# Filter weights queued ahead of two late tables, one activation table, and a first evacuation shared by two engines, in a spectral filter plus feed-forward kernel

## The chip, the cores and the metric

The kernel runs on one core of a Trainium2 chip. The metric is device microseconds for one execution, lower is better. The "span" of a profile is the part between the first and the last instruction of the core; the time of the same execution is 1.8 to 2.5 us longer in the executions quoted here. A run that is over 1.5% slower than the fastest of its kernel counts as slow: medians and ranges below include it, ratios leave it out, and no profile shown is of such a run. The engines are named as the profile names them: PE is the matrix engine (TensorE), DVE is VectorE, ACT is ScalarE, POOL is GpSimd, SP issues nearly all DMAs. A PSUM bank is one of the eight areas (0 to 7 in the zones of this kernel) that PE writes into and that ACT or DVE empties ("evacuates") before this kernel lets PE use it again.

## The reference, cut to what matters

```python
def reference(A_x, A_w_r, A_w_i, B_x, B_w1, B_b1, B_w2, B_b2):
    def _A_ref(x, w_r, w_i):                      # spectral filter
        X = jnp.fft.rfft2(x.astype(jnp.float32), axes=(-2, -1))
        X = X * (w_r + 1j * w_i)                  # filter weights: 2048 x 321, real and imaginary
        return jnp.fft.irfft2(X, s=(S, D), axes=(-2, -1)).astype(jnp.bfloat16)
    def _B_ref(x, w1, b1, w2, b2):                # feed-forward layer, 640 -> 1536 -> 640
        h = _gelu(jnp.einsum("bsd,df->bsf", x, w1) + b1)
        return jnp.einsum("bsf,fd->bsd", h, w2) + b2
    x = A_x                                       # 1 x 2048 x 640, bfloat16
    xn = _layernorm(x, axis=-1)
    return x + _A_ref(xn, A_w_r, A_w_i) + _B_ref(xn, B_w1, B_b1, B_w2, B_b2)
```

## The kernel before

The Fourier transforms are matrix products with constant tables (`gtab`, `etab`, `mtab` forward; `ntab`, `getab`, `htab` back). The sequence is cut into 16 chunks of 128 rows. A "ring" at the start normalises and transposes the chunks; blocks of chunks then go through the hidden layer (`ps<-xnT,W` in the profile, 128, 256 or 512 columns wide), and in between eight pairs go through forward transform, middle transform, multiplication with the filter weights and inverse transform. The names to know are `Xb` (a forward transform's result, evacuated), `Y` (a middle transform's result, evacuated), `T` (products of `Y` and the weights `Wf`), `Z` (their sums), and `Zs` (a rearranged part of `Z`, the "gather").

The program doesn't write the engines' orders by hand. Every operation gets a priority and a list of engines, a small model of the chip simulates the run, and the order that comes out of it is fixed for each engine. On the chip every engine goes through its own list in that order. No instruction passed a waiting one in front of it: in run 2 below, a copy on DVE that needs no weights starts at 59.23 us, behind products that waited 4.08 us for theirs.

```python
PRIO = {"hps": 10, "gelu": 50, "pb": 70, "pc": 80, "filt": 85, "ipc": 90, "xb": 20, "eps": 60, "fin": 40, "fst": 5}
WARM = 12          # matmuls that only bring PE's clock up
DEPTH = 4          # filter loads in flight at once
# ... cut ...
def schedule(self):
    # ... cut: the model; among the operations that could start now, the highest priority is taken
        t, o = min((c for c in cands if c[0] <= t0 + 0.03), key=lambda c: (-c[1].prio, c[1].seq))
# ... cut: the queue of loads, in program order: x chunks between three slabs of W1 (640 KB each) ...
load_x(0, 1)
load_x(1, 1)
load_w1(0)
load_w1(1)
load_x(2, 2)
load_w1(2)
# ... cut: the other x chunks, tables G, E, M, N, GE ...
load(b2bc[:], ...)                                   # bias broadcast, 160 KB
def load_w(dst, src, nbytes, rate):                  # one filter load waits for the one DEPTH before it,
    few.append(load(dst, src, B_w, nbytes, after=few[-DEPTH:][:1], rate=rate))   # or for the first one
# ... cut: 18 filter loads ...
load(htab[:]..., const["H"], B_h, 524288)            # table H, needed late
# ... cut ...
# the products wait for Y, for all filter loads, and for the end of the ring
t_ops[pair].append(K.op([("dve", ...)], pr, lambda e, _: e.tensor_tensor(out=T, in0=Y, in1=Wf, op=ALU.mult),
    reads=[Y, B_w, B_wpad], writes=[TB], after=ring_ops))
```

## Time and profile before

| what | before |
|---|---|
| time, first session | 164.24 us median of 4 runs |
| span of the profile that is read | 162.5 us |
| PE busy | 151.2 us, 93% |
| PE's largest waits after its first matmul | 2.70, 1.08, 0.81, 0.75, 0.55, 0.52, 0.42 us |

PE is the engine to shorten. Read its timeline as a list of waits: each has a length in brackets and the engine or transfer that ended it. The lines themselves stand in the prediction. One more fact matters for reading every comparison: the kernel before isn't steady. Its runs in four sessions range from 162.2 to 168.1 us with medians of 164.2, 166.2, 165.5 and 165.2. So a kernel is compared only with the runs of its own session.

### The profile page before, as it was taken

What the parts mean: (1) busy time and instruction counts of PE and PEld (TensorE: products, weight loads), DVE (VectorE), ACT (ScalarE), POOL (GpSimd) and SP (SyncE); (2) the same over time, 40 slices, a digit from 0 to 9 for tenths busy, and PEclk for the clock granted to TensorE, in tenths of its full rate; (3) what the DMA queues carried; (4) which work ended last, traced back from release to release, by engine and by line L of the source; (5) the groups of instructions that cost most, each with busy time, mean ns of one, the idle gap of its engine ahead of it and who ended that gap; (6) DMA issues with size and microseconds to landing.
All of it is one profiled execution on the core that took longest, in us unless ns stands there. A gap on an engine that the chain in (4) does not pass through costs nothing.

```text
span 162.5 us, 3629 instructions
## 1 busy us (share of the span) xinstructions
PE 151.2 (93%) x1485; PEld 96.7 (59%) x1485; DVE 122.4 (75%) x263; ACT 77.5 (48%) x156; POOL 30.7 (19%) x33
## 2 busy tenths in 40 slices
PE   6979899999999849889999989899999999999993
PEld 2469887455565333445454657567776667777771
DVE  3687999999964655969494999788999898932221
ACT  3098887786787365797769383333011103100000
POOL 1201211111000000000000000305965833333300
PEclk9999999999999978999999999999999999999999
DMA  4999949999999600005050400101344443111121
GB/s 122 355 380 397 300 127 159 169 70 141 127 103 144 146 4 0 0 4 161 4 161 8 160 0 0 38 6 42 108 138 119 131 155 120 45 40 40 42 74 47
DMA packets 18632, 17.84 MB, mean 110 GB/s; under 512 B 6713, under 2 KB 17337, under 8 KB 18489
## 3 DMA queue, kind: packets, MB, share of 16 engines
q1 hardware_dynamic: 18448, 17.59, 47.9%
q8 instruction: 11, 0.18, 0.5%
q10 hardware_dynamic: 168, 0.04, 0.1%
q14 instruction: 5, 0.03, 0.1%
HBM read 13.69 MB, written 2.62 MB: 100 GB/s over the span
## 4 chain that ended last, share of the span: by engine, by line
PE 60%; DVE 25%; ACT 7%; DMA 5%; issue 2%; SPq 0%; DVEq 0%
PE ps L478 59%; DMA Wf<-in_A_w_i_dram 5%; DVE T L627 4%; DVE stats L573 4%; DVE T L711 3%; DVE T L592 2%; DVE Z L716 2%; ACT Xb L485 2%; ACT Zs L485 2%; DVE Y L623 1%; DVE XW L488 1%; DVE Y L488 1%; PE ps L600 1%; ACT gT L655 1%; DVE T L623 1%
## 5 line engine op out<-in xcount | busy, mean ns | idle before, releaser
L478 PE MATMUL ps<-xnT,W 128*128 128x512 bf16 (+2 forms) x360 | 58.1, 311 | 2.1 <-ACT gT L655 2.0
L478 PE MATMUL ps<-W,gT 128*128 128x320 bf16 x384 | 56.3, 299 | 0.1
L478 PEld LDWEIGHTS ps<-W,gT 128*128 128x128 bf16 x384 | 36.7, 98 | 14.9 <-issue 0.5
L478 PEld LDWEIGHTS ps<-xnT,W 128*128 128x128 bf16 x360 | 29.0, 98 | 20.9 <-ACT gT L655 3.8
L655 ACT ACTIVATE gT<-ps,b1col 128x512 bf16<-128x512 f32 (+2 forms) x72 | 36.2, 549 | 8.4 <-PE ps L478 7.9
L821 POOL TENSOR_TENSOR xo<-xr,b2bc 128x640 f32<-128x640 bf16 x11 | 16.6, 1514 | 23.2 <-DVE ost L834 23.2
L485 ACT ACTIVATE Wf<-ps 128x640 bf16<-128x640 f32 x10 | 6.8, 702 | 27.1 <-PE ps L478 27.1
L821 POOL TENSOR_TENSOR xnT<-xr,xnT 128x640 f32<-128x640 bf16 x5 | 7.8, 1553 | 63.3 <-DVE Z L716 61.4
L834 DVE TENSOR_TENSOR ost<-ps,xo 128x640 bf16<-128x640 f32 (+1 forms) x12 | 9.2, 766 | 13.5 <-PE ps L478 13.4
L573 DVE BATCH_NORM_STATS2 stats<-XV 128x6 f32<-128x320 bf16 x32 | 14.1, 471 | 2.2 <-DMA XV<-in_A_x_dram 2.2
L711 DVE TENSOR_TENSOR T<-Y,Wf 128x1288 bf16<-128x1288 bf16 x16 | 12.7, 829 | 3.5 <-DMA Wf<-in_A_w_i_dram 3.0
L581 POOL TENSOR_TENSOR rstd<-ve,mhalf 128x2 f32<-128x2 f32 (+1 forms) x9 | 6.1, 681 | 33.8 <-DVE ve L580 33.8
L488 DVE CAST Y<-ps 128x644 bf16<-128x644 f32 x8 | 6.6, 827 | 6.4 <-PE ps L478 6.4
L804 DVE TENSOR_TENSOR Wf<-Wf 128x640 bf16<-128x640 bf16 x16 | 9.8, 642 | 1.4 <-ACT Wf L485 1.3
L809 DVE TENSOR_TENSOR Wf<-Wf 128x640 bf16<-128x640 bf16 x16 | 10.4, 676 | 0.1
L485 ACT ACTIVATE Zs<-Z 128x128 bf16<-128x128 bf16 (+1 forms) x32 | 6.0, 261 | 9.2 <-DVE Z L716 9.2
L488 DVE CAST XV<-ps 128x640 bf16<-128x640 f32 x8 | 6.6, 823 | 4.9 <-PE ps L478 4.9
L478 PE MATMUL ps<-ntab,Z 64*128 64x128 bf16 x128 | 5.4, 228 | 4.8 <-ACT Xb L485 4.0
L485 ACT ACTIVATE Xb<-ps 128x640 bf16<-128x640 f32 x10 | 8.5, 881 | 1.2 <-PE ps L478 1.2
L478 PEld LDWEIGHTS ps<-ntab,Z 64*128 64x128 bf16 x128 | 4.0, 100 | 8.1 <-ACT Xb L485 6.3
L478 PE MATMUL ps<-etab,XW 128*128 128x160 bf16 (+1 forms) x128 | 8.6, 234 | 0.0
L478 PE MATMUL ps<-getab,XV 128*128 128x160 bf16 (+1 forms) x128 | 8.6, 233 | 0.0
(48 smaller groups left out, 147.8 us busy)
## 6 DMA issues: line engine op xcount, KB each, us to landing
W<-in_B_w_dram SPq DMA_DIRECT2D x6, 640.0 KB, 5.1
xr<-in_A_x_dram SPq DMA_DIRECT2D x16, 160.0 KB, 2.3
out_dram<-ost SPq DMA_DIRECT2D x15, 160.0 KB, 1.8
XV<-in_A_x_dram SPq DMA_DIRECT2D x7, 320.0 KB, 9.1
Wf<-in_A_w_r_dram SPq DMA_DIRECT2D x7, 160.5 KB, 6.0
Wf<-in_A_w_i_dram SPq DMA_DIRECT2D x7, 160.5 KB, 5.4
gtab<-c_G SPq DMA_DIRECT2D x1, 512.0 KB, 8.4
htab<-c_H SPq DMA_DIRECT2D x1, 512.0 KB, 11.6
```

The costliest lines, as they stand in the source:

```text
L478: ins = e.matmul(o_, lhsT=lw, rhs=rh, start=st, stop=sp_)
L485: return e.activation(dst(), src(), ACT.Copy, scale=scale)
L488: return e.tensor_copy(dst(), src())
L573: K.op([("dve", 0.4)], 100 - c, lambda e, _, c=c, h=h: e.bn_stats(stats[:, c, 6 * h:6 * h + 6], view(XV, c * D + H2 * h, [[1, H2]])), read ...
L581: K.op([("pool", 0.75)], 100 - c, lambda e, _, a=a, b=b: e.tensor_tensor(out=rstd[:, a:b], in0=ve[:, a:b], in1=mhalf[:, a:b], op=ALU.pow), ...
L627: K.op([("dve", dve_us(4 * n, 2))], prf, lambda e, _, op=op, x1v=x1v, xfv=xfv, o_=o_, o0=o0, o1=o1, n=n: e.tensor_tensor(out=xfv(o_, [[D, ...
L655: K.op([("act", act_us(s1 - s0, 1))], pr + PRIO["gelu"], lambda e, _, s0=s0, s1=s1, fc=fc, hps=hps: e.activation(gT[:, fc, s0:s1], ps(hps. ...
L711: t_ops[pair].append(K.op([("dve", dve_us(4 * KP, 2))], pr, lambda e, _, k=k, Y=Y, TB=TB, pair=pair: e.tensor_tensor(out=view(TT, TB.slot ...
L804: K.op([("dve", dve_us(D, 2))], pr + 2, lambda e, _, k=k, op=op, yo=yo, y2=y2: e.tensor_tensor(out=view(Wf, Y2 + y2.slot * 2 * D + (H2 - 1 ...
L809: K.op([("dve", dve_us(D, 2))], pr + 3, lambda e, _, k=k, op=op, y2=y2, yf=yf: e.tensor_tensor(out=view(Wf, YF + yf.slot * 2 * D + (D - 1) ...
L821: K.op([("pool", pool_us(640))], 50, lambda e, _, c=c, xr=xr, xov=xov: e.tensor_tensor(out=xov(0, D), in0=halves(xrt[:, xr.slot, :]), in1= ...
L834: os_ops.append(K.op([("dve", dve_us(H2 * len(hs)))], 95, lambda e, _, a=a, b=b, hs=hs, xov=xov, fps=fps, os_=os_: e.tensor_tensor(out=hal ...
```

## The change

The intent: take the waits out of PE's row. The 18 filter loads go ahead of table H and the bias, and the first four of them go without waiting. A GELU on one column of a constant (128x1), as ACT's first instruction, loads the one table that both GELU and copy use. The first two chunks are transposed in two parts (three and two column blocks), one emptied by DVE and one by ACT. Two warm-up matmuls go, the second chunk's statistics wait for the first chunk's variance, and all priorities and bank zones get new values, which rearranges every engine's order. The core of the diff:

```diff
-PRIO = {"hps": 10, "gelu": 50, "pb": 70, "pc": 80, "filt": 85, "ipc": 90, "xb": 20, "eps": 60, "fin": 40, "fst": 5}
+PRIO = {'hps': 37.4, 'gelu': 82.7, 'pb': 120.8, 'pc': 154.1, 'filt': 90.5, 'ipc': 148.4, 'xb': 65.5, 'eps': 59.4, 'fin': 18.3, 'fst': 17.7}
...
-WARM = 12
+WARM = 10
...
-        load(b2bc[:], bass.AP(tensor=b2v.tensor, offset=b2v.offset, ap=[[0, 128], [1, D]]), B_b2b, 163840)
...
-            few.append(load(dst, src, B_w, nbytes, after=few[-DEPTH:][:1], rate=rate))
+            few.append(load(dst, src, B_w, nbytes, after=few[-DEPTH:][:1] if len(few) >= DEPTH else [], rate=rate))
...
-        load(htab[:].rearrange("p a b -> p (a b)"), const["H"], B_h, 524288)
+        load(htab[:].rearrange("p a b -> p (a b)"), const["H"], B_h, 524288, after=few[-2:-1])
+        load(b2bc[:], bass.AP(tensor=b2v.tensor, offset=b2v.offset, ap=[[0, 128], [1, D]]), B_b2b, 163840, after=few[-2:-1])
...
+        K.op([("act", 1.3)], 300, lambda e, _: e.activation(mhalf[:, 8:9], mhalf[:, 0:1], ACT.Gelu_apprx_tanh), reads=[B_mh], writes=[Buf("table")])
...
-                     reads=[B_x[c]], writes=[B_st])
+                     reads=[B_x[c]], writes=[B_st], gate=ve_ops[0:1])
...
-                tps = Buf(f"tps{c}", psum, 1, ZONE["tps"])
+                for ja, jb, engs in ((0, 5, "da"),) if c > 1 else ((0, 3, "d"), (3, 5, "a")):
+                    tps = Buf(f"tps{c}_{ja}", psum, 1, ZONE["tps"])
```

Cut: new zones, a smaller constant `mhalf`, the first GELU's dependence on the warm-ups (dropped), other chunks staged early (`STAGED`), `AHEAD`, `XRAT`, and the body of the split transposes.

> **What bounds the kernel now.** I read the page first, then the chain of waits, then the timeline of the places where the matrix engine stood still, then the DMA queue's own timeline. The page:
>
> ```profile
> span 162.5 us, 3629 instructions
> ...
> PE 151.2 (93%) x1485; PEld 96.7 (59%) x1485; DVE 122.4 (75%) x263; ACT 77.5 (48%) x156; POOL 30.7 (19%) x33
> ...
> PE   6979899999999849889999989899999999999993
> ...
> DMA  4999949999999600005050400101344443111121
> ```
>
> PE is busy 93% of the span and no other engine passes 75%, so the floor is PE's own work; what can be won is its idle time, 162.5 - 151.2 = 11.3 us, plus matmuls that are warm-up only or run slow. The row of slices shows the dips: the first three slices, slices 14 and 15 (53 to 61 us), and the last. Each dip in the timeline:
>
> ```profile
> 1.58 5.30 PE L478 MATMUL ps<-gT 128*128 128x512 bf16 x12 [1.58 <-DVE gT L548]
> ...
> 8.66 1.28 ACT L655 ACT_TABLE_LOAD   x1
> ...
> 10.38 4.08 PE L478 MATMUL ps<-xnT,W 128*128 128x128 bf16 x70 [1.08 <-ACT gT L655]
> ...
> 54.40 1.57 DVE L711 TENSOR_TENSOR T<-Y,Wf 128x1288 bf16<-128x1288 bf16 x2 [3.00 <-DMA Wf<-in_A_w_i_dram]
> ...
> 59.10 1.04 PE L478 MATMUL ps<-ntab,Z 64*128 64x128 bf16 x16 [2.70 <-ACT Xb L485]
> ...
> 60.28 2.04 PE L478 MATMUL ps<-xnT,W 128*128 128x512 bf16 x5
> ...
> 62.93 1.25 PE L478 MATMUL ps<-xnT,W 128*128 128x512 bf16 x5
> ```
>
> Columns: start, us, engine and line, instruction, in brackets the idle time before it and its releaser. Three things are to be seen. PE works on warm-up matmuls until 6.88 us, then a second load of an activation table (8.66 to 9.94) holds the first GELU, and PE, whose PSUM banks are full, stands 1.08 us. VectorE had the first filter product ready to start at 51.4 and waited 3.00 us for the last filter weight; the inverse transform behind it reached PE 2.70 us late. After that gap the same five matmuls cost 2.04 us instead of 1.25: PE's clock had dropped. The other PE gaps are 0.42 (at 16.7), 0.52 and 0.55 (69 to 70), 0.75 (94.7) and 0.81 (103.9), all behind an evacuation by ACT or DVE. Ahead of the first matmul lie 1.58 us, and after the last one 2.64 us (159.86 to 162.5). The sum, 11.05, is nearly all of the 11.3.
>
> Why the weights were late, from the queue:
>
> ```profile
> 11.87 0.68 SPq L473 DMA_DIRECT2D Wf<-in_A_w_r_dram  x1
> 12.59 0.43 SPq L473 DMA_DIRECT2D htab<-c_H  x1
> 23.01 1.84 SPq L473 DMA_DIRECT2D Wf<-in_A_w_r_dram  x3
> ...
> 43.05 3.05 SPq L611 DMA_TRANSPOSE xnT<-T  x2
> 46.14 1.07 SPq L473 DMA_DIRECT2D Wf<-in_A_w_i_dram  x2
> ```
>
> The first weight load was issued at 11.87; the second waited for its landing, until 23.01; and the last two were issued at 46.14, behind the last pair of transposes, and landed 54.2.
>
> **What the Trainium skill says.** "ScalarE: Activation LUTs", section "What ACT_TABLE_LOAD costs", gives about 1283 ns for a load, whatever the set; the trace has two loads of mean 1283 ns. The same page, "Table sets: the hidden batching unit", says that cheap functions such as copy are in every set, so one GELU load can serve the copies too. "TensorE: Matmul & The Clock Gate", section "What's actually happening", says that the array runs at half clock until about 3.4 us of activity, and again after an idle window. The trace agrees on both rates (5.30 / 12 = 442 ns for a 512-column matmul at the start, 216 ns later), but here 2.70 us of idleness was enough; that measurement decides. "SBUF — State Buffer", "Who interferes with whom": a DVE operation with two SBUF inputs and a GpSimd one that reads SBUF exclude each other; the DVE combines of line 809 take 476 to 1683 ns here, the long ones while POOL works.
>
> **The change part by part.** Span figures; the time outside the span, 164.29 - 162.5 = 1.8 us, I take as fixed.
>
> Start. Twelve warm-up matmuls become ten: 2 x 0.43 = 0.86 us off PE. That pays only if the first transpose is ready by 5.86. The first chunk's statistics now run alone: 3.09 + 2 x 0.39 + 0.11 + 0.1 gives the variance at about 4.1, GpSimd's power 0.6 (from the 4.97 to 5.57 of the profile), behind it the second chunk's statistics until 4.9, the normalisation 0.4: ready about 5.3. So the transposes start at 5.86 instead of 6.89: 1.03 us. Two engines share the copy of the first chunk; the first 128-column matmul then starts near 6.95 instead of 8.01. The table is loaded about 1.1 to 2.4 us, when ACT has nothing else, and the second load, 1.28 us, disappears; with it the 1.08 us of PE. Together 2.1 us. Part is given back: twenty-four GELUs of 277 ns (4.99 / 18) and two copies of 0.65 are 8.0 us of ACT against 120 x 0.058 + 1.4 = 8.4 us of PE, so they run neck and neck, and the second and third slabs of W1, which landed by about 8.8 and 11.4 us (my estimate from the landing of the x chunk between them, 9.69, at 0.38 MB per us), are now needed at about 9 and 11.5. I take back 0.7. Net 1.4 us.
>
> Filter weights. Four loads are now issued without a wait, at about 10 to 12.5 us, and the late table (0.52 MB) and the bias broadcast (0.16 MB) go behind: 0.69 MB / 0.38 = 1.8 us of queue ahead of them disappears, and so does the hole at 22 to 24 us, when the DMA engines were 0.09 busy. The order shows the last filter load issued before the last pair of transposes, not after it: that pair waits for chunks 14 and 15, normalised at 41.0 to 42.0 in the old trace. So the last load is issued by about 41 and, at the 7 us to landing that such loads took late in the old queue, lands by 48 to 50. Its first use moves also: DVE loses about 1 us in the ring (one 0.73 us evacuation moves to ACT, the copies shrink) and starts earlier, so the product would be ready at about 50 instead of 51.4. Remaining wait 0 to 1 us. Moreover PE now has between the first middle transform and the first inverse one: five hidden-layer groups of 1.08, two forward transforms of 0.95 and two middle ones of 0.67, 8.6 us, against a vector chain of 0.8 (Y) + 1.57 (products) + 0.8 (copy) + 0.8 (Z) + 1.0 (gathers) = 5.0. So PE should not stop even if a weight is 2 us late. Worth: the 2.70 us of idleness and the slow matmuls after it, (1.04 - 0.62) + (0.42 - 0.28) + (2.04 - 1.25) = 1.35. Sum 4.05 us.
>
> Order. New priorities and zones change every later interleaving. The steady pattern per pair is three groups of 1.08 plus 0.95, 0.67 and 0.83, 5.7 us of PE, against 5.2 us of DVE, and between a middle and its inverse transform PE has 6.8 us against a chain of 5.3. The 0.52, 0.55 and 0.75 should mostly go. The last pair has only 1.07 + 0.83 + 3.2 = 5.1 us of PE to cover 5.1, so the 0.81 is likely to stay. The last output transform comes 28 matmuls (3.7 us) earlier in PE's order, while DVE was 94 to 96% busy from 110 to 140: new small gaps are likely. I count 1.0 us net.
>
> Sum: 1.4 + 4.05 + 1.0 = 6.5 us; 164.3 - 6.5 = 157.8 us.
>
> **Rivals.** (a) The weights are still late: between 24 and 54 us DMA was busy throughout (share 0.9 to 1.3 in every stretch of 4 us) and carried only 99 to 164 MB per ms of narrow rows and transposes, so reordering may only redistribute. Against it: two transposes go behind, the hole is filled, and PE's filling is 3 us longer. If it held, 2 of the 4 us go: about 160. (b) VectorE becomes the bound of the last third, where POOL lengthens its operations; every position of the output transform that I counted has 0 to 2 us of slack. For it, the 95%; against it, PE never waited there before and ends with six groups of 3.5 us that need nothing new. It would give back 1 to 3 us: 159 to 161. (c) All stalls go: 151.2 - 0.86 - 1.35 + 1.58 + 2.64 + 1.8 = 155.0, the best that this work allows. (d) The gain at the start is lost because the ring of chunks is set by DVE, continuously busy from 15.8 to 44.9 us. PE has other work there, so work done earlier still shortens the end; I give this little weight.
>
> **Range and chances.** From 155.0 (c) to about 160.5 (a, or the worse half of b). Two per cent under 164.29 is 161.0; to miss it more than half of the gains must fail together, and the largest two are independent. Faster 0.92, within 0.07, slower 0.01.
>
> **What would show each step.** One table load in the trace, over by 2.5 us, and the 1.08 us before the 128-column matmuls gone; first transpose at about 5.9. The last filter load landing before 50, no DMA wait of DVE before its first product, and no PE gap over 1 us between 50 and 70, with five 512-column matmuls at 1.25 us or less everywhere. PE's busy time near 149 us, idle near 7. The prediction is wrong if a wait for DVE appears before output transforms after 100 us, if PE shows half-clock matmuls beyond 8 us, or if its idle time in the middle stays above 3 us.

## The result, and the profile after

| | before | after |
|---|---|---|
| time, same session, median | 164.24 us (162.24 to 166.82, 4 runs) | 158.19 us (157.06 to 158.71, 4 runs) |
| span of the profile | 162.5 us | 155.0 us |
| ratio of fast runs | 1 | 0.966 (0.956 to 0.977) |

The change makes the kernel faster by 3.4%. A ratio here and below is the mean time of one kernel's fast runs over the mean of the other's fast runs of the same rounds, so it isn't quite the ratio of the medians beside it.

The page of the changed kernel: the two dips of PE in the middle are gone, and the busy stretch of the DMA row ends with the 13th slice (50 us) instead of in the 14th (52.8 to 56.9 us before).

```profile
span 155.0 us, 3617 instructions
...
PE 147.4 (95%) x1473; PEld 95.5 (62%) x1483; DVE 124.4 (80%) x277; ACT 73.1 (47%) x144; POOL 30.3 (20%) x33
...
PE   5699999999999999999999999999999999999993
...
DMA  4999949799999000019141400002533442211111
```

This trace has 1473 matmul records against 1483 weight loads, so some matmul records are missing and PE's 147.4 us is a little low; a second execution of the same kernel with all 1483 recorded has 149.0 us, which is the figure that the prediction names.

PE's timeline after (start, us, engine and line, instruction, in brackets the wait before it and what ended it). These are all its waits, apart from gaps of 0.16 us put down to "issue" where a matmul's record is missing; the second line has no wait and shows where the first transposes are:

```profile
1.59 4.20 PE L477 MATMUL ps<-gT 128*128 128x512 bf16 x10 [1.59 <-DVE gT L547]
5.86 0.45 PE L602 MATMUL ps<-ident,T 128*128 128x128 bf16 x5
7.60 0.72 PE L477 MATMUL ps<-xnT,W 128*128 128x128 bf16 x10 [1.29 <-DMA W<-in_B_w_dram]
...
12.17 2.00 PE L477 MATMUL ps<-xnT,W 128*128 128x128 bf16 x33 [0.38 <-ACT gT L657]
...
59.20 0.62 PE L477 MATMUL ps<-ntab,Z 64*128 64x128 bf16 x16
...
119.79 1.08 PE L477 MATMUL ps<-getab,XV 128*128 128x160 bf16 x16 [0.24 <-DVE ost L836]
122.41 1.07 PE L477 MATMUL ps<-getab,XV 128*128 128x160 bf16 x16 [0.18 <-DVE Wf L487]
```

Three things are to be seen. The first inverse transform (59.20) has no bracket: the 2.70 us are gone. So are the four waits of 0.5 to 0.8 us behind it, and two small ones appear after 119 us. And the start still has a wait, 1.29 us long, but another transfer ends it: the first slab of W1.

ACT's timeline shows the table. There is one load, at the start, and the GELU's first instruction follows the copies with no load between:

```profile
1.14 1.28 ACT L550 ACT_TABLE_LOAD   x1 [1.14 <-PEq L856]
...
8.91 0.18 ACT L558 ACTIVATE b1col<-ps 128x12 f32<-128x12 f32 x1
9.12 3.20 ACT L657 ACTIVATE gT<-ps,b1col 128x128 bf16<-128x128 f32 x12
```

The DMA queue after: four filter loads at once at 10.59, the last two at 39.16, ahead of the last pair of transposes. Table H waits for the last filter load but one to land and is issued at 47.10:

```profile
10.59 3.13 SPq L472 DMA_DIRECT2D Wf<-in_A_w_r_dram  x4
22.36 2.22 SPq L472 DMA_DIRECT2D Wf<-in_A_w_i_dram  x4
...
39.16 1.07 SPq L472 DMA_DIRECT2D Wf<-in_A_w_i_dram  x2
40.28 4.25 SPq L613 DMA_TRANSPOSE xnT<-T  x2
47.10 0.34 SPq L472 DMA_DIRECT2D htab<-c_H  x1
```

On DVE the products start as soon as `Y` is there, with no wait:

```profile
50.23 0.83 DVE L487 CAST Y<-ps 128x644 bf16<-128x644 f32 x1 [0.90 <-PE ps L477]
51.15 1.57 DVE L713 TENSOR_TENSOR T<-Y,Wf 128x1288 bf16<-128x1288 bf16 x2
```

**Where the 7.5 us of span went.** To share them out I cut both traces at one place: the end of the group of PE that holds the last 128-column hidden-layer matmul, 17.13 + 2.70 = 19.83 us before and 16.37 + 2.95 = 19.32 after. Ahead of the cut PE does the same work in both, except for the two warm-ups fewer, which are part of the change, and five 256-column matmuls more after, as the groups up to the cut show (busy us and mean ns of one behind the bar). Before:

```profile
L478 PE MATMUL ps<-xnT,W 128*128 128x256 bf16 x18 | 2.1, 273 | 0.0
```

After:

```profile
L477 PE MATMUL ps<-xnT,W 128*128 128x256 bf16 x23 | 2.7, 273 | 0.0
```

Five of them are 5 x 2.7 / 23 = 0.6 us. On equal work the start of this execution is therefore 19.83 - (19.32 - 0.6) = 1.1 us faster, and the rest is 142.7 us before and 136.3 after, 6.4 us faster. (7.5 us is more than the 6.1 between the medians: the profiled execution of the changed kernel is the fastest of its four.) Which part of the change brought the 6.4, and whether the 1.1 is there in every execution, the experiments show.

### The profile page after: what moved, and what is told of

Its sections match the earlier page's. It is cut to its first block, busy times and chain, and to the rows that moved or that the text cites. A ratio compares the mean times of both kernels' runs of the same rounds, so it can differ in the third digit from the quotient of the medians.

```text
span 155.0 us, 3617 instructions
## 1 busy us (share of the span) xinstructions
PE 147.4 (95%) x1473; PEld 95.5 (62%) x1483; DVE 124.4 (80%) x277; ACT 73.1 (47%) x144; POOL 30.3 (20%) x33
## 4 chain that ended last, share of the span: by engine, by line
PE 74%; DVE 14%; DMA 4%; issue 3%; ACT 2%; SPq 1%
PE ps L477 73%; DVE Wf L806 4%; DMA W<-in_B_w_dram 4%; DVE Wf L811 4%; DVE ost L836 3%; DVE Wf L487 2%; ACT gT L657 2%; PE ps L602 1%; DVE xnT L792 1%; SPq L472 1%; ACT xnT L484 0%; ACT b1col L558 0%
## 5 line engine op out<-in xcount | busy, mean ns | idle before, releaser
L477 PE MATMUL ps<-xnT,W 128*128 128x512 bf16 (+2 forms) x350 | 56.6, 306 | 2.7 <-DMA W<-in_B_w_dram 1.3
L477 PEld LDWEIGHTS ps<-xnT,W 128*128 128x128 bf16 x360 | 28.5, 98 | 19.7 <-issue 1.8
L484 ACT ACTIVATE Wf<-ps 128x640 bf16<-128x640 f32 x9 | 6.2, 704 | 25.9 <-PE ps L477 25.9
L811 DVE TENSOR_TENSOR Wf<-Wf 128x640 bf16<-128x640 bf16 x16 | 11.8, 775 | 0.1
L806 DVE TENSOR_TENSOR Wf<-Wf 128x640 bf16<-128x640 bf16 x16 | 10.4, 682 | 0.1
L484 ACT ACTIVATE Xb<-ps 128x640 bf16<-128x640 f32 x8 | 7.1, 890 | 4.3 <-PE ps L477 4.3
L484 ACT ACTIVATE XW<-ps 128x640 bf16<-128x640 f32 x12 | 8.3, 704 | 1.3 <-PE ps L477 1.1
L484 ACT ACTIVATE XV<-ps 128x640 bf16<-128x640 f32 x9 | 6.2, 703 | 5.6 <-PE ps L477 5.6
L487 DVE CAST Xb<-ps 128x640 bf16<-128x640 f32 x8 | 7.1, 883 | 1.2 <-PE ps L477 1.2
L477 PEld LDWEIGHTS ps<-etab,XW 128*128 128x128 bf16 (+1 forms) x128 | 5.4, 95 | 4.2 <-ACT Xb L484 0.4
```

Source lines behind the costliest of these rows:

```text
L477: ins = e.matmul(o_, lhsT=lw, rhs=rh, start=st, stop=sp_)
L484: return e.activation(dst(), src(), ACT.Copy, scale=scale)
L487: return e.tensor_copy(dst(), src())
L806: K.op([("dve", dve_us(D, 2))], pr + 2, lambda e, _, k=k, op=op, yo=yo, y2=y2: e.tensor_tensor(out=view(Wf, Y2 + y2.slot * 2 * D + (H2 - 1 ...
L811: K.op([("dve", dve_us(D, 2))], pr + 3, lambda e, _, k=k, op=op, y2=y2, yf=yf: e.tensor_tensor(out=view(Wf, YF + yf.slot * 2 * D + (D - 1) ...
```

## The experiments

All edits are made after the scheduling model has run, so that every compute engine keeps the order of the kernel it comes from, and only the thing named differs (in the sixth run the model isn't told of the two warm-ups, to the same end). All kernels gave correct results. The diffs are shortened; `...` and comments stand for what is left out. There were three sessions: runs 1 to 4, 5 to 8, and 9 to 12, each on one chip. My theory: the early weights bring about 4 us by themselves, the new order about 1, the start (table, warm-ups, shared evacuation) about 1.4. The rival theories: the weights are hidden by the new order anyway; or the start is bound by something else, which takes the place of what was removed.

### 1. The old kernel with the new queue

```diff
+        # after scheduling: SP's order is the new kernel's, the filter loads wait as there
+        K.order["sp"] = ... + few[:11] + tr[:2] + few[11:14] + tr[2:4] + few[14:16] + tr[4:6] + few[16:] + tr[6:] + [h_op, b2_op] + ...
+        for i, o in enumerate(few):
+            o.deps = [few[i - DEPTH]] if i >= DEPTH else []
+        h_op.deps, b2_op.deps = [few[-2]], [few[-2]]
```

> The kernel before with only the DMA queue of the changed one (four filter loads unblocked, late table and bias behind them, last filter loads ahead of the last transposes); the order of every compute engine is pinned and is the same as before. Theory (the late filter weights cost the old order 2.7 us of PE idleness and 1.35 us of slow matmuls): no DMA wait before the first filter product, no PE gap before the first inverse transform, no 2.04 us group; the time falls by about 4.0 us, ratio to before about 0.976. Rival (the gain comes from the new interleaving, and the weights only move the wait elsewhere): the time falls by less than 1 us, ratio above 0.994, and a PE gap of 1.5 us or more stays between 50 and 70 us.

Measured: 160.88 us (160.12 to 161.76, 6 runs) against 166.23 (162.88 to 167.65, 11 runs) of the kernel before, ratio 0.982 (0.975 to 0.990); span 158.4. The ratio is nearer to 1 than the medians are because it leaves out the slower half of the old kernel's scattered runs. In PE's timeline between 60 and 105 us, these are the waits; the first one is not the first inverse transform, which has none:

```profile
64.97 0.62 PE L478 MATMUL ps<-ntab,Z 64*128 64x128 bf16 x16 [0.52 <-ACT Xb L485]
...
66.25 1.25 PE L478 MATMUL ps<-xnT,W 128*128 128x512 bf16 x5 [0.54 <-ACT gT L655]
...
90.68 0.62 PE L478 MATMUL ps<-ntab,Z 64*128 64x128 bf16 x16 [0.76 <-ACT Xb L485]
...
99.87 0.63 PE L478 MATMUL ps<-ntab,Z 64*128 64x128 bf16 x16 [0.81 <-DVE Zs L488]
```

The wait of 2.70 us and the slow matmuls behind it are gone, the four small waits of the old order are all still there (0.52 + 0.54 + 0.76 + 0.81 = 2.6 us), and the cut lies at 19.86 us as before. So the rest is 158.4 - 19.86 = 138.5 us: the queue alone is worth 142.7 - 138.5 = 4.1 us. That is a difference of two single executions, and the old kernel's vary: in run 4 below, which has the old queue too, the wait was 2.10 us and no slow matmuls followed, and against its rest (160.8 - 20.06 = 140.7) the queue is worth 2.2 us. The ratio of fast runs, 0.982, is 3.0 us of their mean of 164.0 (1.7 to 4.2). Which of the queue's three moves did it (four loads without a wait, table and bias behind, the last loads ahead of the last transposes) was not taken apart.

The changed kernel's rest is 136.3, so the new order is worth 138.5 - 136.3 = 2.3 us (unrounded: 138.54 - 136.27), close to the difference between the small waits here (2.6) and those of the changed kernel (0.42).

### 2. The new kernel with the old queue

```diff
+        # after scheduling: SP's order is the old kernel's, the filter loads wait as there
+        K.order["sp"] = ... + [b2_op, few[0], h_op] + few[1:6] + tr[:2] + few[6:10] + tr[2:4] + few[10:14] + tr[4:6] + few[14:16] + tr[6:] + few[16:] + ...
+        for i, o in enumerate(few):
+            o.deps = [few[max(0, i - DEPTH)]] if i else []
+        h_op.deps, b2_op.deps = [], []
```

> The changed kernel with only the DMA queue put back to the old one; compute orders pinned and equal to the changed kernel's. The first filter product should wait about 3 us for the last weight again (start near 54.3). Theory (the new order has 8.6 us of PE work where the vector chain needs 5.0, so it hides most of a late weight): PE loses 1 to 1.5 us, since two copies of later pairs stand behind the delayed product on VectorE, and its clock does not drop; ratio to the changed kernel about 1.007. Rival (early weights are the whole gain of the middle): PE idle 2.5 us or more there plus slow matmuls, about 4 us slower, ratio to the changed kernel about 1.025.

Measured: 164.56 us (162.98 to 165.82, 6 runs), ratio 1.002 (0.991 to 1.012); span 163.3. Without the early weights the ratio shows nothing of the gain. My theory had said that PE has 8.6 us of other work to cover a late weight. Three engines in order show why it can't use it. DVE's timeline:

```profile
57.74 1.57 DVE L713 TENSOR_TENSOR T<-Y,Wf 128x1288 bf16<-128x1288 bf16 x2 [4.08 <-DMA Wf<-in_A_w_i_dram]
59.23 0.87 DVE L487 CAST Xb<-ps 128x640 bf16<-128x640 f32 x1
```

ACT's:

```profile
60.91 0.31 ACT L484 ACTIVATE Zs<-Z 128x128 bf16<-128x128 bf16 x1 [4.58 <-DVE Z L718]
61.13 0.87 ACT L484 ACTIVATE Xb<-ps 128x640 bf16<-128x640 f32 x1
```

PE's:

```profile
62.05 1.29 PE L477 MATMUL ps<-Xb,mtab 64*64 64x322 bf16 x16 [4.03 <-ACT Xb L484]
```

DVE waits 4.08 us for the last weights. Behind the products in its order stands a copy `Xb`, which needs no weights at all; behind the gather `Zs` in ACT's order stands another. PE's next middle transform, which needs no weights of its own either, was released only by such a copy, 4.03 us after PE had run out of work. From the products' start to that transform it is 62.05 - 57.74 = 4.3 us, and in the changed kernel with early weights 55.47 - 51.15 = 4.3 us as well, without a wait (PE was busy until 55.43): PE's cover there is just used up. In this run a late weight cost PE what it was late. PE's clock dropped after this wait too (1.29 us for a middle transform of 0.74, 2.32 for five matmuls of 1.25).

The size of the loss is not the old queue's alone. The last weights landed at 57.4 us here, at 54.2 in the kernel before. And of the 8.3 us between this span and the changed kernel's, only 5.7 lie behind the cut (4.03 of waiting, 1.6 of slow matmuls). The other 2.6 lie ahead of it (cut at 21.92 us): PE was at half clock already in the transposes before its wait for the slab (0.72 us for five, where 0.45 is usual), and stayed there behind it:

```profile
8.06 1.23 PE L477 MATMUL ps<-xnT,W 128*128 128x128 bf16 x10 [1.43 <-DMA W<-in_B_w_dram]
```

### 3. The new kernel with two table loads

```diff
+        K.order["act"].remove(early)          # the early GELU; its dependents no longer wait for it
```

> The changed kernel without the early GELU on ACT, so that the table is loaded twice again; all orders else the same. Theory (PE and ACT run neck and neck in the first blocks, so ACT's delay of 1.28 us reaches PE and then the end): second table load near 9.1 us, first GELU at 10.4 instead of 9.12, 0.9 to 1.3 us slower, ratio to the changed kernel about 1.007. Rival (something later, the chunks that VectorE sets or the W1 slabs, makes PE wait anyway and absorbs it): less than 0.4 us slower.

Measured: 158.98 us (158.59 to 159.69, 6 runs), ratio 0.971 (0.964 to 0.977); span 157.5. The changed kernel's own runs in the other sessions have medians of 158.2 to 158.8, so the early table is worth between 0.2 and 0.8 us, less than the 0.9 to 1.3 expected; no more can be said across sessions. Its cut lies at 21.51 us. Where PE waited at the start, again the slab of W1 came last, and PE ran the matmuls behind it at half clock (1.23 us for ten, where 0.72 is usual):

```profile
8.12 1.23 PE L477 MATMUL ps<-xnT,W 128*128 128x128 bf16 x10 [1.74 <-DMA W<-in_B_w_dram]
```

### 4. The old kernel with one table load

```diff
+        K.order["act"].insert(1, early)       # GELU on one column of a constant, as ACT's first computation
```

> The kernel before with only the early GELU added, so that one table load is left, all orders pinned. Theory: the 1.08 us gap of PE at 9.3 to 10.4 us disappears and the end comes about 1.1 us earlier, ratio to before 0.993. Rival (the ring of chunks on VectorE sets the pace to 46 us, and the filter weights the next point): the gap at 10 us disappears, but the wait for the filter weights, which does not move, takes it back: PE idle before the first inverse transform grows from 2.7 to 3.5 us or more and the time is the same within 0.4 us.

Measured: 166.04 us (163.31 to 166.95, 6 runs) against 166.23 of the kernel before, ratio of the fast runs 1.014 (1.004 to 1.024): no gain. PE's timeline at the start:

```profile
8.17 1.28 PE L479 MATMUL ps<-xnT,W 128*128 128x128 bf16 x20 [0.43 <-DMA W<-in_B_w_dram]
10.02 2.28 PE L479 MATMUL ps<-xnT,W 128*128 128x128 bf16 x38 [0.57 <-DMA W<-in_B_w_dram]
12.74 1.95 PE L479 MATMUL ps<-xnT,W 128*128 128x128 bf16 x32 [0.44 <-DMA W<-in_B_w_dram]
```

The wait of 1.08 us for the table is gone, and in its place PE waits for each of the three slabs of W1, 0.43 + 0.57 + 0.44 = 1.4 us. The cut lies at 20.06 us, not earlier than the 19.83 of before. The slabs landed later in this execution than in that one (8.04, 9.88 and 12.60 us against 6.85, 8.83 and 11.53), so run 1, which has both table loads, is the fairer partner: there they landed at 7.86, 9.70 and 12.41, and the cut is 19.86. So with slabs as late as these, the table hid a wait for the slabs. The rival on record was another one, a growing wait for the filter weights, and it is out: that wait was shorter here than before, and PE kept its clock behind it.

```profile
58.74 0.62 PE L479 MATMUL ps<-ntab,Z 64*128 64x128 bf16 x16 [2.10 <-ACT Xb L486]
```

### 5. The new kernel again, as a control

> The changed kernel itself, unchanged, so that it stands on the same chip and beside the same runs of the kernel before as the next three. Every theory: ratio to before 0.96 to 0.97; one table load; no DMA wait before the first filter product; blocks 0 and 1 of the hidden layer end near 19.3 us.

Measured: 158.78 us (157.94 to 159.37, 6 runs) against 165.47 (163.48 to 167.47, 12 runs), ratio 0.967 (0.963 to 0.972); span 157.6. This execution has two waits in the ring that the first one hasn't (0.65 and 1.10 us, the second for a DMA transpose), so even with the same program single spans differ by 2.6 us.

### 6. Twelve warm-up matmuls again

```diff
-        ... [(ps(B_wp.slot, 0, 512), gT[:, 0, 0:128], gT[:, 0, 128:640], True, True)] * WARM)
+        ... [(ps(B_wp.slot, 0, 512), gT[:, 0, 0:128], gT[:, 0, 128:640], True, True)] * (WARM + 2))
```

> The changed kernel with twelve warm-up matmuls instead of ten, all orders pinned. The prediction's term: the two are worth 0.86 us on PE, so 0.8 us slower. Rival, from the trace after (the first 128-column matmul waited 1.29 us for the first slab of W1, until 7.60): the two matmuls run in a time in which PE waits anyway, the first 128-column matmul moves from 7.6 to about 8.0, and the kernel is 0 to 0.4 us slower.

Measured: 158.67 us (157.65 to 160.40, 6 runs) against the control's 158.78. The first hidden-layer matmul starts at 7.87 after a wait of 1.40 us for the slab. The two warm-ups run in time in which PE waits anyway; taking them out is worth nothing.

### 7. Both parts of the first transposes emptied by DVE

```diff
+        for nm in ("xnT0", "xnT1"):           # ACT's half moves behind DVE's half, in DVE's order
+            K.order["act"].remove(o); o.eng = "dve"; K.order["dve"].insert(K.order["dve"].index(d) + 1, o)
```

> The changed kernel with both parts of the first two chunks' evacuation on VectorE, one after the other, instead of shared with ACT; all orders else pinned. If the sharing matters, the first 128-column matmul comes 0.3 us later and the kernel is 0.3 us slower. If the first slab of W1 is what the matmul waits for, both parts are done by 7.0 us, the matmul starts at 7.6 as before and the time is the same within 0.2 us.

Measured: 158.67 us (157.66 to 159.85, 6 runs), the same as the control. The first hidden-layer matmul starts at 8.13, after 1.60 us for the slab. Sharing the evacuation isn't what the time depends on.

### 8. The first slab of W1 in two loads, and the bias column earlier

If the slab's landing is what the start waits for, half of the slab should let PE begin.

```diff
-            load(W1[:, j, :, :], w1v[:, :, 512 * j:512 * j + 512], B_w1s[j], 655360)      # j = 0
+        half.emit = lambda e, _: e.dma_start(W1[:, 0, :, 0:256], w1v[:, :, 0:256])        # the first two groups wait for this
+        slab0.emit = lambda e, _: e.dma_start(W1[:, 0, :, 256:512], w1v[:, :, 256:512])
+        # and the bias transpose and its copy move right behind the first chunk's transposes
```

> The changed kernel with two additions meant to pull the start forward: the first slab of W1 comes in two loads of half the columns, and the bias transpose with its copy stands right behind the first chunk's transposes instead of behind the second chunk's. Theory (after the table load is gone the start waits for the first slab, and the GELUs for the bias column at 9.1 us): first 128-column matmul near 7.0, first GELU near 8.0 instead of 9.12, the end 0.5 to 1.0 us earlier. Rival (chunks 2 and 3, whose x lands at 10.2 us, and the later slabs set the pace of the first 20 us): blocks 0 and 1 still end near 19.3 and the time is the same within 0.3 us.

Measured: 157.36 us (156.93 to 159.22, 6 runs), ratio 0.961 (0.954 to 0.967); span 156.0. The first hidden-layer matmul starts at 7.00, but a wait of 1.38 us for another slab follows, and the cut lies at 19.98 us, no earlier than in the control's execution (19.70). By the trace the rival holds; by the times it is 1.4 us faster than the control. The two don't agree, so I ran it again, with its parts apart and more rounds (runs 9 to 12).

### 9 to 12. The control again, the half slab alone, the bias column alone, both

> Control for the three runs beside it: the changed kernel itself. Both theories: 158.2 to 159.2 us median, ratio to the kernel before 0.966 to 0.972.

> The changed kernel with its first slab of W1 loaded as two halves of the columns; the bias column stays where it is. If the landing of the first slab is what the start waits for and work done earlier counts at the end: the first 128-column matmul starts 0.6 to 1.2 us earlier than in the control, and the median is 0.5 to 1.2 us below the control's. Rival, later slabs take over the wait: blocks 0 and 1 end within 0.3 us of the control's and the median is within 0.5 us of it.

> The changed kernel with only the bias transpose and its copy moved right behind the first chunk's transposes. It takes no wait away that ends last (the slab's landing does), so both theories expect the control's median within 0.4 us; if it is over 0.6 us below, the bias column was a bound of the start that I did not see.

> The half slab and the early bias column together, as in the run before that had 157.36 us. If that was a real gain: 157.0 to 157.9 us, 0.7 us or more below the control of this call, with intervals of the ratios that do not overlap. Rival, the gain was the scatter of six runs: within 0.5 us of the control.

| run | median us (range), 6 runs | ratio to before | first hidden matmul, wait ahead | cut | span |
|---|---|---|---|---|---|
| 9 control | 158.53 (156.59 to 159.54) | 0.964 (0.956 to 0.971) | 8.27, 1.91 | 20.61 | 156.4 |
| 10 half slab | 157.30 (157.17 to 157.62) | 0.961 (0.957 to 0.965) | 6.81, 0.48 | 19.41 | 155.4 |
| 11 bias column | 158.46 (157.78 to 159.25) | 0.968 (0.963 to 0.972) | 7.97, 1.54 | 20.38 | 156.4 |
| 12 both | 157.46 (157.11 to 157.69) | 0.961 (0.958 to 0.965) | 7.07, 0.35 | 19.78 | 155.7 |

The kernel before had 165.22 us (163.06 to 168.06, 12 runs). By the medians the half slab brings the 1.2 us, the bias column nothing. On fast runs alone, which leave out the control's two above 159.4, the means are 157.8, 157.3, 158.4 and 157.4: the half slab is 0.5 us below the control, 1.1 below run 11, which has the whole slab too. So the gain lies somewhere between 0.5 and 1.2 us. The page of the control's execution shows the clock that PE was granted, in tenths, by slices of a fortieth of the span:

```profile
PEclk9959999999999999999999999999999999999999
```

That is slow in the third slice, 7.8 to 11.7 us. In its PE timeline the first ten hidden-layer matmuls cost 1.22 us instead of 0.72:

```profile
8.27 1.22 PE L477 MATMUL ps<-xnT,W 128*128 128x128 bf16 x10 [1.91 <-DMA W<-in_B_w_dram]
...
10.40 5.05 PE L477 MATMUL ps<-xnT,W 128*128 128x128 bf16 x80
```

The half slab's page and timeline:

```profile
PEclk9999999999999999999999999999999999999999
```

```profile
6.81 0.73 PE L477 MATMUL ps<-xnT,W 128*128 128x128 bf16 x10 [0.48 <-ACT xnT L484]
...
9.44 2.41 PE L477 MATMUL ps<-xnT,W 128*128 128x128 bf16 x40 [0.84 <-DMA W<-in_B_w_dram]
```

Waiting for a whole slab costs twice: PE waits, and in some executions it loses its clock for the matmuls that follow. Of the six profiled executions with the whole slab, one table and the new queue (the first one and runs 5, 6, 7, 9 and 11), PE waited 1.29, 1.40 and 1.49 us in three and kept its clock; in the other three it waited 1.54, 1.60 and 1.91 us, after 0.4 to 0.8 us of idleness ahead of the transposes that the first three hadn't, and lost it, and their cuts lie at 20.4 to 20.6 us instead of 19.3 to 19.7. With the half slab the wait is cut in two, and none of its three executions lost the clock. That fits the times: all twelve runs of 10 and 12 lie within 157.1 and 157.7 us, and four of the control's six above 158.3. But its fastest run, 156.59, is faster than any of them: the half slab takes the bad starts away, it doesn't better the best one. That the clock makes up the whole 1.2 us I can't show, since only one execution of each run is profiled. My condition for run 12, intervals of the ratios that don't overlap, isn't met either: both ratios use the old kernel's scattered runs as their base. Side by side the kernel with the half slab is the best version found, three times 1.1 to 1.4 us below its control.

What follows for the rest: span minus cut is 135.7 to 136.0 us in the first execution and in runs 3, 6, 7, 8, 9, 10, 11 and 12 alike, though their cuts differ by 2.2 us. Whatever the start loses or wins arrives undiminished at the end; only run 5, with its late transpose, is off.

## Why the prediction was right or wrong

The time, 157.8 predicted and 158.2 measured, and the class were right. The terms of the sum (6.5 us) weren't all: with the 3.0, 0.5 and 2.3 us found below it is 5.8, near the 6.1 between the medians, and that it comes so close is luck, since too small a term for the order made up for the others.

**Filter weights: 4.05 us predicted; 4.1 measured against the execution that the prediction read, 2.2 against run 4's, 3.0 by the fast runs** (run 1). The mechanism was right, and the size where PE waits 2.70 us and loses its clock. Its checks are met too: the last loads issued at 39.16 instead of 46.14 and the last one landed at 47.6 instead of 54.2, no DMA wait of DVE before the products, no wait of PE between 50 and 70 us, no slow matmuls there. Rival (a), weights late all the same, is out.

**The slack behind the weights: wrong, without harm.** "So PE should not stop even if a weight is 2 us late" counted PE's work between two of its instructions (8.6 us) against one chain of DVE (5.0). Run 2 showed that this work isn't to be had: the copies that release it stand behind the products and the gather in the orders of DVE and ACT. The slack was about zero. It did no harm because no weight was late.

**Start: 1.4 us predicted; 1.1, 0.7 and -0.2 measured** in the three executions of the changed kernel (the first one, runs 5 and 9; 19.83 minus the cut, with the 0.6 us of extra work added), 0.5 on average. This term was mis-sized, and its step failed: "Two engines share the copy of the first chunk; the first 128-column matmul then starts near 6.95 instead of 8.01"; it started at 7.60, 8.01 and 8.27. I had worked out when the second and third slabs of W1 land, and took 0.7 us back for them, but hadn't asked for the first one. In the trace that I read it had landed at 6.85 us, just ahead of the 6.95, so asking would have shown no wait. But in the ten other executions with a whole slab, old kernel or new, it landed at 7.46 to 8.14: one trace didn't show how much a landing moves. It came last, and made the two warm-ups (run 6) and the shared evacuation (run 7) worth nothing and hid what the table had cost (run 4). The transposes did start at 5.86 as predicted, and PE then stood. That half-clock matmuls can follow such a wait was not in the sum at all.

**Order: 1.0 us predicted, 2.3 measured** (run 1 against the changed kernel). The waits of 0.52, 0.55 and 0.75 went as predicted. The 0.81, "likely to stay", went too: the cover that I had counted for the last pair, 5.1 us, was right (94.52 - (88.57 + 0.74) = 5.2 us between the last middle and the last inverse transform), but the chain behind it fitted into that, where it had taken 103.95 - (96.62 + 0.75) = 6.6 us before. And the new gaps that I had set against the gain are 0.24 + 0.18 us only.

Of the rivals, (b), VectorE as the bound of the last third, is visible as just these two waits. They are also one of the prediction's own signs of being wrong ("a wait for DVE appears before output transforms after 100 us"); it came true, with 0.42 us. Another, half-clock matmuls beyond 8 us, is absent in the first execution and there in runs 7, 9 and 11. (c), 155.0 us for a kernel without stalls, wasn't reached by any run. (d) had the right idea, a start whose gain is lost, and the wrong agent: not DVE, whose gains and losses ahead of the cut reached the end in full, but the slabs of W1.

## What to carry to other kernels

Before you count the removal of a wait as a gain, list for the instruction behind it all its inputs with their times of landing, the first load too, and from more than one trace: the second latest is what you will wait for. Work that could cover a late transfer counts only if each engine's own order lets its evacuations pass the instruction that waits; otherwise the cover is zero. And put every part of a change back alone, once: a right total here was made of terms too large and one too small.

## What the Trainium skill lacked or had wrong

- "TensorE: Matmul & The Clock Gate", section "What's actually happening": it gives a window of about 3.4 us for losing the clock. Here waits of 1.54 to 1.91 us, with 0.4 to 0.8 us of idleness shortly before, were enough in four executions (runs 3, 7, 9 and 11); waits of 1.29 to 1.49 us, without it, were not in three others; and at the first inverse transform 2.70 us were enough, where 2.10 us in run 4 were not. The page does say that the window runs freely, so that the same program meets it differently; it lacks a figure for how short a single wait can already cost the clock. Whether the wait's length or the idleness before it decided isn't shown.
- "ScalarE: Activation LUTs", section "What ACT_TABLE_LOAD costs": its 1283 ns for a table load agree with the trace (1.28 us). Of the 1380 ns of draining that it adds, nothing is to be seen here: in the kernel before the load ran from 8.66 to 9.94 and the GELU started at 9.95.
- No page has a figure for how much the landing of one and the same load moves between executions: the first slab of W1, issued at 1.65 to 1.67 us each time, landed at 6.85 us in the profile before and at 7.46 to 8.14 in ten others, and it released PE at 7.60, 7.87, 7.97, 8.01, 8.13 and 8.27 us in six executions with the same queue.
- "PSUM — Partial Sum Buffer", section "Engine vs sequencer instructions", says that the queues of ScalarE and VectorE are strictly first in, first out, and the trace agrees. It lacks what follows for evacuations: one that stands behind an instruction waiting for data holds PE up for work that needs none of that data. In run 2, 4.08 us of waiting on DVE became 4.03 us on PE.
